# Block-sparse attention and gated MLP on one core: head 0's first queries transposed in fp32, copied in four chunks

## The chip, the cores and the metric

One core of a Trainium2 chip runs the whole program. The time is the device time of one execution in microseconds (us), the median of several. The engines of the core are named as the profile names them: PE (TensorE, the matrix products, with its weight loads listed as PEld), DVE (VectorE), ACT (ScalarE), POOL (GpSimd) and SP (SyncE, which issues most transfers). Each engine works through its own list of instructions in order, and waits at an instruction until what it needs has been signalled.

## The reference

```python
# attention: q, k, v are [4, 8, 768, 64], blocks of 32
scores = q @ k.T / 8
mask = |block_i - block_j| <= 1, or either block is the first or last,
       or block_j is one of three sampled blocks of block_i
attn = softmax(where(mask, scores, -1e9))
x = (attn @ v), heads side by side: [4, 768, 512]
# gated MLP with a spatial product
h = relu(x @ w_in)                      # 1024 columns
u, v = h[..., :512], h[..., 512:]
v_n = (v - mean(v)) / sqrt(var(v) + 1e-6)
v_s = w_spatial @ v_n + b_spatial       # along the sequence
out = (u * v_s) @ w_out
```

## The kernel before

Sixteen pairs of heads (four of each of the four batches) go through attention, and each batch then through the MLP. For one head the kernel keeps a tile `kq`: rows 0 to 63 hold the transposed keys (columns 0 to 767) and queries (columns 768 to 1535), rows 64 to 127 hold rows that carry the mask, one-hot block numbers under the keys and penalties under the queries. A product of 128 rows then gives score and mask at once. ACT turns each block of scores into exponentials (`a_all`), PE multiplies them with the values (`vv`), which carry a column of ones for the sum, and DVE divides.

Sequence positions are laid out so that each of the 128 partitions holds six neighbouring positions; a "chunk" is one of these six, and a transpose of two chunks of 64 columns at a time gives 128 rows: the first chunk in rows 0 to 63 and the second in rows 64 to 127 of the PSUM tile.

The schedule is written by hand: the order of the code is the order on each engine. Pair 0's heads are treated apart, since nothing can run before their data is there. Their first four chunks are loaded by `load` through ACT's queue (keys, then queries, of head 0), the rest through SP's. `cast` converts the staged fp32 tile `st_k` or `st_q` to the bf16 tile `nat`; for the first four chunks it also reorders them, so that one transpose yields chunks 0 and 2 and the other chunks 1 and 3, and rows 0 to 63 of the PSUM tile hold chunks 0 and 1 side by side (the first third of the queries, 256 columns) and rows 64 to 127 chunks 2 and 3. `head` issues these transposes, with `ident` as identity, and `split0` copies one half (`t` = 0 or 1) out of PSUM into `kq` on DVE. `make_identity` fills and selects on POOL.

`mask_rows(ps, t, copy, ...)` multiplies the penalty table `bm` with the one-hot rows for a third `t` of the queries and copies the result (64 rows, 256 columns) into head 0's `kq`. `rows(heads, columns, engine)` copies mask rows from head 0 to other heads. `filler` issues small products of no use that keep PE active. The step `casts` lets POOL work off `ORDER`, the casts of pair 1, 2, 3 and so on, and issues the loads that are four entries ahead; a staging buffer is loaded again when its cast is done.

Then the slots begin. Each `qk_unit` issues the score products of one block into one of two PSUM buffers `sc` and one exponential on ACT; the very first, of head 0, is issued in two halves (`ps` and `ps_f`), each with its own exponential. Other steps (transposes of later pairs, value products, later the MLP) are hung to slots by number.

Of the kernel before, what the change touches and what calls it, by code (L numbers as in the profile page):

```python
# [10 lines left out]
FP32 = mybir.dt.float32  # L11
# [15 lines left out]
def kernel(  # L27
# [16 lines left out]
    nc = tc.nc  # L44

    B, H, S, D = q.shape
# [16 lines left out]
    TC = NCH // NT  # L63
    TW = TC * 128
# [5 lines left out]
    const = ctx.enter_context(tc.tile_pool(name="const", bufs=1))  # L70
    work = ctx.enter_context(tc.tile_pool(name="work", bufs=1))
    psum = ctx.enter_context(tc.tile_pool(name="psum", bufs=1, space=bass.MemoryType.PSUM))
    ctx.enter_context(tc.manual_schedule())

    ident = const.tile([128, 128], BF16)
    warm = const.tile([128, 128], BF16)
    w_in_t = const.tile([128, NDM, DFF], BF16)
    w_out_t = const.tile([128, NDH, DM], BF16)
# [4 lines left out]
    kq = const.tile([128, H, 2 * S], BF16, name="kq")  # L83
    NVV = 6
    vv = [const.tile([128, 2, NCH, VA], BF16, name=f"vv{s}") for s in range(NVV)]
    MR = slice(D, KR)
    MX = slice(D, 128)
    K_, Q_ = slice(0, S), slice(S, 2 * S)

    def qcols(t0, n=1):  # L90
        return slice(S + t0 * TW, S + (t0 + n) * TW)


    st = {}
# [6 lines left out]
    H0, H1, BOTH = slice(0, 1), slice(1, 2), slice(0, 2)  # L101
    ALLC, C01, C03, C45 = slice(0, NCH), slice(0, TC), slice(0, 2 * TC), slice(2 * TC, NCH)
# [12 lines left out]
    def nat0_view():  # L115
        return nat[0].rearrange("p c h d -> p (c h d)").rearrange("p (h x) -> p h x", h=2)

    def cast(p, nm, eng, hs=BOTH, cs=ALLC):
        if nm == "v":
            dst = vv[p % NVV][:, hs, cs, 0:D]  # L120
        else:
            if p not in nat:
                nat[p] = work.tile([128, 2 * NCH, 2, D], BF16, tag="nat", bufs=4, name="nat")
            c0 = 0 if nm == "k" else NCH
            dst = nat[p][:, c0 + cs.start:c0 + cs.stop].rearrange("p c h d -> p h c d")[:, hs]
        src = st[nm, p].rearrange("p h (c d) -> p h c d", d=D)[:, hs, cs]
        if p == 0 and nm != "v":
            dst = nat0_view()[:, hs, (c0 + cs.start) * D:(c0 + cs.stop) * D]
            if cs is not C45:
                dst = dst[:, 0].rearrange("p (i t d) -> p t i d", t=2, d=D)  # L130
                src = src[:, 0].rearrange("p (t i) d -> p t i d", t=2)
            else:
                dst = dst.rearrange("p h (c d) -> p h c d", d=D)
        if eng is nc.scalar:
            nc.scalar.activation(out=dst, in_=src, func=AF.Copy)
        else:
            eng.tensor_copy(out=dst, in_=src)  # L137
# [23 lines left out]
    def iota(out, pattern, base, mult):  # L161
        nc.gpsimd.iota(out, pattern=pattern, base=base, channel_multiplier=mult,
                       allow_small_or_imprecise_dtypes=True)
# [2 lines left out]
    iota(edge[MR], [[0, 1]], 1 - NB, 2)  # L166
    iota(hot[MX], [[2, NCH], [2 * NCH, 128]], 1 - BLK, -2 * BLK)
    iota(col[MR], [[0, NR], [1, NB]], 0, 0)
    make_identity(nc, ident)
    for s in range(NVV):  # L170
        nc.gpsimd.memset(vv[s][:, :, :, D:VA], 1.0)
    nc.gpsimd.memset(mhalf, -0.5)
    nc.gpsimd.memset(kq[0:D, 1, 0:TW], 0.0)

    wps = psum.tile([128, 512], FP32, tag="av", bufs=2)

    def filler(n, to):
        for _ in range(n):
            nc.tensor.matmul(out=to[:, 0:128], lhsT=warm, rhs=warm, start=True, stop=True)
# [28 lines left out]
    PL, DV = nc.gpsimd, nc.vector  # L208
# [4 lines left out]
    def act_copy(o, i):  # L213
        nc.scalar.activation(out=o, in_=i, func=AF.Copy)
# [21 lines left out]
    def rows(hs, cs, eng=nc.vector):  # L236
        src = kq[MX, 0:1, cs].to_broadcast([MX.stop - MX.start, hs.stop - hs.start, cs.stop - cs.start])
        if eng is nc.scalar:
            nc.scalar.activation(out=kq[MX, hs, cs], in_=src, func=AF.Copy)
        else:  # L240
            eng.tensor_copy(out=kq[MX, hs, cs], in_=src)

    cast(0, "k", nc.scalar, H0, C03)
    act_copy(kq[MX, 0, K_], kq[MX, 1, K_])
    cast(0, "q", PL, H0, C03)
    cast(0, "k", PL, H0, C45)
    cast(0, "k", PL, H1)
    cast(0, "q", PL, H1, C03)
# [4 lines left out]
    def moe_tag():  # L253
        moe_tags.rotate(1)
        if moe_tags[0] in held:
            moe_tags.rotate(1)
        return moe_tags[0]

    def bank(nm="ps", tag=None):
        return psum.tile([128, 1024], BF16, tag=tag or moe_tag(), bufs=2 if tag else 1, name=nm)  # L260
# [7 lines left out]
    def mask_rows(ps, t, copy, h=0, rs=slice(0, KR)):  # L268
        nc.tensor.matmul(out=ps[:, 0:TW], lhsT=bm[rs], rhs=kq[rs, h, t * TW:(t + 1) * TW],
                         start=True, stop=True)  # L270
        copy(kq[MX, 0, qcols(t)], ps[0:MX.stop - MX.start, 0:TW])


    def head(ps, h, c0, n, at=0):
        for i in range(0, n, 2):
            nc.tensor.transpose(out=ps[:, at + i * 64:at + (i + 2) * 64],
                                in_=nat0_view()[:, h, (c0 + i) * D:(c0 + i + 2) * D],
                                identity=ident)

    def split0(ps, h, c0, n, t, copy=dve_copy):  # L280
        w = n * 64
        copy(kq[0:D, h, c0 * 128 + t * w:c0 * 128 + (t + 1) * w], ps[t * D:(t + 1) * D, 0:w])

    K4, K2, Q4 = (0, 2 * TC), (2 * TC, NCH - 2 * TC), (NCH, 2 * TC)
# [3 lines left out]
    rows(slice(3, 4), K_)  # L288
    filler(FILL2[0], wps)
    mask_rows(psum.tile([128, 1024], FP32, tag="sc", bufs=2, name="mq"), 0, act_copy, 1)  # L290
    rows(slice(2, 3), slice(0, 512), nc.scalar)
    filler(FILL2[1], wps)
    psq = bank("psq", "av")
    head(psq, 0, *Q4)
    split0(psq, 0, *Q4, 0)
    split0(ps0, 0, *K4, 1)
    filler(FILL2[2], wps)
    mask_rows(psum.tile([128, 512], FP32, tag=moe_tag(), bufs=1, name="mq"), 1, act_copy, rs=MR)
    split0(psq, 0, *Q4, 1)
    rows(slice(4, 6), K_)  # L300
    rows(H1, qcols(0, 2), PL)
    rows(slice(2, 3), slice(512, S), PL)

    ORDER = ("k1 q1a v00 v01 k2 q2a v1 k3 q3a v2 q1b q2b r v3 q3b q0c w00 w01 w02 w03 w10 w12 w11 w13").split()
    PIECE = {"k": {}, "v": {}, "q": {}, "a": {"cs": C01}, "b": {"cs": C25}, "c": {"cs": C45},
# [592 lines left out]
```

## Time and profile before

| what | value |
|---|---|
| median of 3 runs | 210.62 us (210.41 to 210.62) |
| the profiled execution | 210.04 us, of which its span is 208.3 us |
| PE busy | 201.0 us (97%) |
| ACT busy | 168.4 us (81%) |
| DVE busy | 146.8 us (70%) |
| POOL busy | 89.4 us (43%) |
| granted TensorE clock | 1.00 |

The span is the time from the first to the last recorded instruction; some 1.7 us of the execution lie around it. A view of the profile either lists groups of instructions (line, engine, operation, output and input tiles, shapes, count, busy time and the mean of one in ns, idle time before them with what ended it) or instructions in order of time (start, length, what). The chain of waits follows from the last instruction back to what released it, again and again. Matmuls are pipelined: one lasts longer than the distance to the next.

### The profile page before, as it was taken

The page shows a single profiled execution, that of the slowest core. Times are in us where ns is not written, and L with a number is a line of the kernel's source. Part 1 is how long each engine was busy: PE and PEld are TensorE (multiplying, and loading weights), DVE is VectorE, ACT ScalarE, POOL GpSimd, SP SyncE. Part 2 cuts the span into 40 slices and gives each one's busy share as a digit, 9 for nine tenths or more (in the row PEclk, how much of TensorE's full clock was granted, in tenths as well). Part 3 has the DMA queues.
Part 4 walks back from the last instruction along what each step waited for, and adds up shares of the span by engine and source line. Part 5 has one row for each costly group of instructions (what it writes and reads, how often), then busy time and mean ns, then how long its engine had stood idle before and what let it go on. Part 6 is the DMA issues. An engine that isn't in the chain of part 4 may idle for free.

```text
span 208.3 us, 5489 instructions
## 1 busy us (share of the span) xinstructions
PE 201.0 (97%) x2203; PEld 138.0 (66%) x2225; DVE 146.8 (70%) x315; ACT 168.4 (81%) x222; POOL 89.4 (43%) x186
## 2 busy tenths in 40 slices
PE   6899999999999999999999999999999999999993
PEld 6599888777766776667556676667665567445551
DVE  6888776989876766575975585456875666576871
ACT  6899999999999999989899878889899884266021
POOL 6888989767927964006757600006210000013000
PEclk9999999999999999999999999999999999999999
DMA  5999899999999999499987920499402010610016
GB/s 143 338 362 357 275 383 270 206 247 389 253 253 308 259 300 208 139 199 386 292 176 206 139 41 0 164 189 335 75 0 41 0 37 4 250 57 0 0 70 232
DMA packets 53053, 39.48 MB, mean 190 GB/s; under 512 B 33956, under 2 KB 47652, under 8 KB 53028
## 3 DMA queue, kind: packets, MB, share of 16 engines
q1 hardware_dynamic: 52596, 38.74, 70.0%
q10 hardware_dynamic: 432, 0.39, 0.6%
q8 instruction: 17, 0.28, 0.5%
q14 instruction: 8, 0.07, 0.1%
HBM read 24.77 MB, written 6.29 MB: 149 GB/s over the span
## 4 chain that ended last, share of the span: by engine, by line
PE 87%; DVE 4%; ACT 4%; DMA 2%; issue 1%; POOL 0%; ACTq 0%
PE ps L428 21%; PE ps_moe L630 17%; PE ps_moe L561 13%; PE ps_av L476 12%; PE ps L415 7%; PE ps_av L458 4%; PE ps_t L561 4%; PE ps_t L630 4%; PE ps_sc L630 2%; ACT a_all L420 2%; DVE stats L594 2%; DVE vn L185 2%; DMA st_q<-in_q_dram 2%; PE ps_sc L561 1%; PE ps L263 1%
## 5 line engine op out<-in xcount | busy, mean ns | idle before, releaser
L431 ACT ACTIVATE a_all<-ps 128x768 bf16<-128x768 f32 x144 | 113.4, 812 | 13.8 <-PE ps L428 6.2
L428 PE MATMUL ps<-kq 128*128 128x512 bf16 (+1 forms) x288 | 70.3, 326 | 0.3
L476 PEld LDWEIGHTS <-a_all 128*128 128x128 bf16 x864 | 46.6, 98 | 19.0
L476 PE MATMUL ps_av<-vv,a_all 128*128 128x65 bf16 x864 | 51.1, 194 | 0.1
L428 PEld LDWEIGHTS <-kq 128*128 128x128 bf16 x288 | 27.9, 97 | 23.6
L137 POOL CAST nat<-st_k 128x256 bf16<-128x256 f32 (+3 forms) x37 | 17.7, 509 | 38.7 <-DMA st_k<-in_k_dram 38.7
L420 ACT ACTIVATE a_all<-ps 128x1024 bf16<-128x1024 f32 x35 | 33.5, 1027 | 0.3
L630 PE MATMUL ps_moe<-w_spt,vn 128*128 128x512 bf16 (+1 forms) x144 | 33.1, 325 | 0.0
L598 POOL TENSOR_SCALAR std<-mv 128x3 f32<-128x3 f32 (+1 forms) x9 | 3.4, 376 | 48.7 <-DVE mv L595 48.5
L661 DVE TENSOR_TENSOR sb<-ps_moe,b_row 128x512 f32<-128x512 f32 x18 | 12.4, 690 | 14.5 <-PE ps_moe L630 14.2
L630 PE MATMUL ps_moe<-xt,w_in_t 128*128 128x256 bf16 (+1 forms) x108 | 21.7, 299 | 0.2
L415 PE MATMUL ps<-kq 128*128 128x256 bf16 x135 | 20.8, 275 | 0.8 <-DVE kq L211 0.6
L561 PE MATMUL ps_moe<-w_in_t,xt 128*128 128x512 bf16 x65 | 20.2, 378 | 0.2
L137 POOL CAST vv<-st_v 128x256 bf16<-128x256 f32 (+2 forms) x37 | 18.5, 533 | 3.9 <-DMA st_v<-in_v_dram 3.8
L137 POOL CAST nat<-st_q 128x256 bf16<-128x256 f32 (+2 forms) x41 | 19.2, 496 | 1.6 <-DMA st_q<-in_q_dram 1.5
L561 PE MATMUL ps_moe<-w_out_t,un 128*128 128x512 bf16 x64 | 19.4, 378 | 0.2
L441 DVE TENSOR_TENSOR xn<-ps_av,rc 128x384 bf16<-128x384 f32 (+1 forms) x36 | 18.5, 513 | 1.4 <-DVE rc L440 0.2
L664 DVE TENSOR_TENSOR un<-sb,un 128x512 bf16<-128x512 f32 x24 | 17.4, 727 | 1.5
L630 PEld LDWEIGHTS <-vn 128*128 128x128 bf16 x192 | 15.5, 97 | 4.4
L594 DVE BATCH_NORM_STATS2 stats<-vn 128x6 f32<-128x512 bf16 x24 | 16.5, 688 | 1.5 <-ACT vn L589 0.9
L211 DVE COPY osb<-ps_moe 128x512 f32<-128x512 f32 x12 | 8.3, 689 | 11.2 <-PE ps_moe L561 9.3
L211 DVE COPY kq<-tt 64x1536 bf16<-64x1536 bf16 x24 | 15.4, 641 | 0.6 <-DMA tt<-nat 0.2
(94 smaller groups left out, 241.6 us busy)
## 6 DMA issues: line engine op xcount, KB each, us to landing
out_dram<-osb SPq DMA_DIRECT2D x23, 256.0 KB, 2.1
st_k<-in_k_dram SPq DMA_DIRECT2D x15, 384.0 KB, 4.6
st_v<-in_v_dram SPq DMA_DIRECT2D x15, 384.0 KB, 6.2
st_q<-in_q_dram SPq DMA_DIRECT2D x12, 384.0 KB, 4.9
ws_f<-in_moe_w_spatial_dram SPq DMA_DIRECT2D x6, 384.0 KB, 5.5
w_f<-in_moe_w_in_dram SPq DMA_DIRECT2D x8, 256.0 KB, 6.3
w_f<-in_moe_w_out_dram SPq DMA_DIRECT2D x4, 256.0 KB, 5.4
st_q<-in_q_dram SPq DMA_DIRECT2D x3, 256.0 KB, 6.9
```

Of the source, the lines that this page charges most:

```text
L137: eng.tensor_copy(out=dst, in_=src)
L211: nc.vector.tensor_copy(out=o, in_=i)
L415: nc.tensor.matmul(out=ps[:, at:at + n * TW], lhsT=kq[:, h, ci * 128:(ci + 1) * 128], rhs=kq[:, h, qcols(t0, n)], start=True, stop=True)
L420: nc.scalar.activation(out=out, in_=ps, func=AF.Exp, scale=0.125)
L428: nc.tensor.matmul(out=ps[:, n0:n1], lhsT=kq[:, j % H, ci * 128:(ci + 1) * 128], rhs=kq[:, j % H, S + n0:S + n1], start=True, stop=True)
L431: nc.scalar.activation(out=a_ref["h", j][:, ci, :], in_=ps[:, 0:S], func=AF.Exp, scale=0.125)
L441: nc.vector.tensor_tensor(out=out, in0=ps[:, :, 0:D], in1=rc[:, 0:n].to_broadcast([128, n, D]), op=ALU.mult)
L476: nc.tensor.matmul(out=av_ref[j][:, qc, :], lhsT=a_ref["h", j][:, ci, qc * 128:(qc + 1) * 128], rhs=vv[p % NVV][:, h, ci, :], start=(ci == ...
L561: nc.tensor.matmul(out=ref["ps"][:, 0:w], lhsT=lhs(i), rhs=rhs(i), start=(i == 0), stop=(i == n - 1))
L594: nc.vector.bn_stats(out=stats, in_=self.vn[:, tcc, :])
L630: nc.tensor.matmul(out=o.rearrange("p (c t) -> p c t", c=n), lhsT=lhs(i)[:, (d0 + x) * 128:(d0 + x + 1) * 128], rhs=rhs(i), start=(i == 0) ...
L664: nc.vector.tensor_tensor(out=self.in_place(*area), in0=sb, in1=self.in_place(*area), op=ALU.mult)
```

## The change

The fp32 identity `ident_f` is made first and copied to the bf16 `ident` on POOL; the clearing of head 1's first query columns in `kq` moves ahead of the memsets of `vv`. Head 0's first four query chunks are no longer cast by POOL. PE transposes them from the staged fp32 tile `st_q`, two neighbouring chunks at a time, into an fp32 PSUM tile `psq`, and four copies of one chunk each (64 rows, 128 columns, `q_part`) bring them to `kq`: chunks 0 and 2 by DVE, 1 and 3 by ACT. The second `mask_rows` stands right behind the first, in an `sc` buffer. ACT's copy of 512 columns of mask rows to head 2 goes, and POOL's copy to that head covers all 768 columns instead of the last 256.

```diff
     ident = const.tile([128, 128], BF16)
+    ident_f = const.tile([128, 128], FP32)
...
-    make_identity(nc, ident)
+    make_identity(nc, ident_f)
+    nc.gpsimd.tensor_copy(out=ident, in_=ident_f)
+    nc.gpsimd.memset(kq[0:D, 1, 0:TW], 0.0)
     for s in range(NVV):
         nc.gpsimd.memset(vv[s][:, :, :, D:VA], 1.0)
     nc.gpsimd.memset(mhalf, -0.5)
-    nc.gpsimd.memset(kq[0:D, 1, 0:TW], 0.0)
...
     cast(0, "k", nc.scalar, H0, C03)
     act_copy(kq[MX, 0, K_], kq[MX, 1, K_])
-    cast(0, "q", PL, H0, C03)
     cast(0, "k", PL, H0, C45)
...
     mask_rows(psum.tile([128, 1024], FP32, tag="sc", bufs=2, name="mq"), 0, act_copy, 1)
-    rows(slice(2, 3), slice(0, 512), nc.scalar)
+    mask_rows(psum.tile([128, 1024], FP32, tag="sc", bufs=2, name="mq"), 1, act_copy, 1, MR)
     filler(FILL2[1], wps)
-    psq = bank("psq", "av")
-    head(psq, 0, *Q4)
-    split0(psq, 0, *Q4, 0)
+    psq = psum.tile([128, 512], FP32, tag="av", bufs=2, name="psq")
+    for i in range(TC):
+        nc.tensor.transpose(out=psq[:, i * 128:(i + 1) * 128],
+                            in_=st["q", 0][:, 0, 2 * i * D:2 * (i + 1) * D], identity=ident_f)
+
+    def q_part(c, copy):
+        r = c % 2 * D
+        copy(kq[0:D, 0, S + c * 128:S + (c + 1) * 128],
+             psq[r:r + D, c // 2 * 128:(c // 2 + 1) * 128])
+
+    q_part(0, dve_copy)
+    q_part(1, act_copy)
     split0(ps0, 0, *K4, 1)
     filler(FILL2[2], wps)
-    mask_rows(psum.tile([128, 512], FP32, tag=moe_tag(), bufs=1, name="mq"), 1, act_copy, rs=MR)
-    split0(psq, 0, *Q4, 1)
+    q_part(2, dve_copy)
+    q_part(3, act_copy)
     rows(slice(4, 6), K_)
     rows(H1, qcols(0, 2), PL)
-    rows(slice(2, 3), slice(512, S), PL)
+    rows(slice(2, 3), K_, PL)
```

## The prediction, made before the changed kernel had run

> **What bounds the kernel now.** I read the chain of waits first, because it says which work ends last and where it passes from engine to engine; then the busy time by stages; then the timeline of the first 12 us, which is all that the edits touch. The stages (columns: stretch, its length, busy time and instructions of each engine, granted clock, DMA share, GB/s):
>
> ```profile
> 4.50:6.10 1.60, 1.03 (x8) 0.53 (x9) 0.93 (x4) 1.06 (x3) 1.36 (x4) 1.00 0.82 239
> 6.10:11.00 4.90, 4.08 (x40) 2.88 (x41) 4.31 (x12) 4.89 (x7) 4.61 (x9) 1.00 1.04 349
> 11.00:40.00 29.00, 28.83 (x454) 25.72 (x457) 23.17 (x58) 28.66 (x31) 26.38 (x42) 1.00 1.08 311
> ```
>
> From 11.0 us on PE (first number) hardly rests: 28.83 of 29.00 us here, and 1.1 us of idle in all from 11 to 203 us. From 6.1 to 11.0 it is ACT (fourth) that never rests, 4.89 of 4.90. So a shift of ACT's first exponential moves everything behind it. The chain in the first 11 us (start, us, what):
>
> ```profile
> 1.14 3.19 DMA st_q<-in_q_dram
> 4.34 0.06 issue
> 4.39 0.57 POOL nat L137
> 4.97 0.04 issue
> 5.01 0.30 PE psq L276 x2
> 5.31 0.02 issue
> 5.34 0.30 DVE kq L211
> 5.63 0.04 issue
> 5.68 0.41 PE ps L407 x2
> 6.08 0.02 issue
> 6.11 1.09 ACT a_all L410 x2
> 7.19 3.77 ACT a_all L420 x4
> 10.96 0.04 issue
> 11.01 0.60 PE ps L415 x4
> ```
>
> Head 0's first queries land at 4.33; GpSimd casts, PE transposes, DVE copies, PE multiplies, and the first exponential starts at 6.11. That start is the quantity to predict; a handover costs 0.02 to 0.06 us.
>
> **The change part by part.** The unknown is X, the time from PE's start on the queries (4.39 as GpSimd's before, the landing being the same) to the end of both fp32 transposes.
>
> *The cast goes.* 0.57 us of GpSimd and one handover of 0.04 leave the chain.
>
> *The transposes become fp32.* No fp32 matmul is in the trace. Lower end: the bf16 pair, 0.30. In the built program the fp32 transpose is one instruction without the separate weight load that each bf16 one has, so I count its load as unhidden. A load takes 0.097 (first row below), a product follows the last by 0.056 (the row of eight: 0.61 less the 0.22 of one, over 7), and 0.16 (0.22 - 0.056) is the last one's latency. One load and one product each: X = 2 x 0.153 + 0.16 = 0.47. Upper end, four unhidden passes each: 2 x 4 x 0.153 + 0.16 = 1.38. I take 0.47, nearest to the bf16 row, since a transpose only moves data. The Trainium skill, "TensorE: Matmul & The Clock Gate", section Terms, says that Trainium2's weight loads and matmuls have a transpose mode that is four times faster for FP32; by it the sum goes with 0.47, and the passes end would not occur; no row here shows it.
>
> ```profile
> L428 PEld LDWEIGHTS <-kq 128*128 128x128 bf16 x288 | 27.9, 97 | 23.6
> 9.51 0.61 PE L263 MATMUL ps<-ident,nat 128*128 128x128 bf16 x8
> L211 DVE CAST kq<-mq 64x256 bf16<-64x256 f32 x1 | 0.4, 419 | 0.0
> L214 ACT ACTIVATE kq<-mq 64x256 bf16<-64x256 f32 x2 | 0.8, 377 | 0.5 <-PE mq L269 0.5
> 4.57 0.61 ACT L239 ACTIVATE kq<-kq 64x512 bf16<-64x512 bf16 x1
> 6.35 1.21 POOL L241 COPY kq<-kq 64x512 bf16<-64x512 bf16 x2
> ```
>
> *Four chunk copies for two copies.* The old 64x256 bf16 copy took 0.284; the new ones read fp32. DVE: 0.419 for 256 columns (CAST row), 0.689 for 512 (the osb copies), so 1.05 ns a column and 0.284 for 128. ACT: 0.377 for 256, and 0.595 against 1.027 for the exponentials of 512 and 1024 columns, 0.84 ns a column, so 0.269. The division looks parallel, but in the built program each copy waits for the one before it: chunk 1 (ACT) for DVE's chunk 0, chunk 2 for ACT, chunk 3 for DVE. The first exponential stands behind chunk 3 on ACT. With t = 4.39 + X: chunk 0 ends at t + 0.03 + 0.284, chunk 1 at t + 0.62, chunk 2 at t + 0.95, chunk 3 runs from t + 0.99. ACT starts the next instruction, if it waits for nothing, 0.1 before the last ends (the mask copy at 4.29 lasts 0.38, the row copy behind it starts at 4.57), so the first exponential starts at t + 0.99 + 0.17 = t + 1.16 = 5.55 + X. The scores are not later: chunk 1 lets PE start at t + 0.67, and 0.43 (6.11 - 5.68) on makes t + 1.10. Against 6.11 the shift is X - 0.56: -0.26, **-0.09**, +0.82 for the three X. On DVE, `split0` of the keys fits into the wait for chunk 1, and chunk 2 ends at 5.34 + X = 5.81 instead of 6.15, so what is queued behind (the 0.56 row copy, the later halves) comes sooner, not later. PE's products for the third exponential now wait for chunk 3 instead of DVE's copy (6.15): with X = 0.47 it ends at 4.86 + 1.26 = 6.12; they take 0.60, and that exponential starts at 7.08 at the earliest.
>
> *Second mask product and ACT's row copy.* The product moves from 5.34 to just behind the first (3.97); its copy, 0.377 on ACT, follows at about 4.57, where the row copy of 0.61 was, and ends by 4.95, before chunk 1 at 5.20. Cost nothing; the cover is PE's and ACT's wait for the queries, and without it 0.38.
>
> *GpSimd's row copy grows from 256 to 768 columns.* It took 0.40; 768 take 0.83 (the same copy at 25.54) to 1.3 (256 and 512 columns here took 0.40 and 0.86). The cast of head 1's queries ends at 6.29 as before, held by its DMA, so rows run 6.31 to 7.8 or 8.5 instead of to 7.56. The next cast waited for its DMA until 7.79: late by 0 to 0.7. Behind it stand pair 1's casts, which PE's transposes use at 9.40 (keys) and 9.75 (queries; their cast ended at 8.96), and the transfers that need those buffers back. At most 0.2 reaches PE at 9.75; ACT has some 0.2 in hand there. I take nothing.
>
> *Identity.* Fill and select once more in fp32, then a 128x128 copy (0.29, as the 128x128 cast): about 3.16 instead of 2.79, wanted by the key transposes at 3.62. The `kq` fill ends at about 3.5, wanted at 3.97. Nothing; uncovered it would be up to 0.4. The count memsets behind end by 4.2, and GpSimd's next cast waits for a DMA.
>
> Sum: -0.09 on the profiled execution's 210.04 (span 208.3 and 1.74 around it). The median of the three runs is 210.62, 0.58 above that execution; the same shift gives **210.5**.
>
> **The rivals.**
> - *fp32 takes several passes, unhidden.* X = 1.38, the first exponential at 6.93, +0.82: 211.4. For it: four bytes a value, and the one-instruction form. Against: overlapped, four passes would be 8 x 0.063 (the load pitch in a row of eight, 0.54 for 8) + 0.16 = 0.66, only +0.10. Slower by 0.42 begins at X = 0.98. The Trainium skill, "FP8 and Floating Point Precision", section TensorE Precision Notes, has true FP32 take four passes; it does not say this of transposes.
> - *fp32 costs what bf16 does.* X = 0.30, -0.26: 210.36. For it: the moving columns are as many. Against: the hidden load that bf16 has.
> - *GpSimd becomes late.* Rows to 8.5, pair 1's casts late by 0.7, and v3's transfer issued later by as much (SP waited for that buffer at 10.22): 0.2 at the transposes and as much again if a weight cast misses; 210.9. For it: GpSimd busy 4.61 of 4.90 us. Against: it waited 0.29 and 0.26 us for DMAs at 11.66 and 14.22, which takes such a lag back, and the first expert weights are cast some 1.3 us before PE uses them at 21.23.
> - *More is gained than the start.* Work that comes earlier fills part of PE's 1.1 us of later idle; -0.5: 210.1. For it: the idle is there. Against: no row ties it to the start.
> - *The copies run side by side, as they are written.* Two rounds of 0.28 instead of four, a start at 5.0 + X and a gain of 0.64 (209.98); the waits in the built program exclude it.
>
> **How the numbers follow.** Forecast 0.38 (210.4 to 210.8), several passes 0.30, bf16's price 0.14, GpSimd late 0.06, more gained 0.12. A measurement here can tell about 0.2%, 0.42 us, from no change. Faster: 0.12 and 0.04 of bf16's price with luck in the idle, 0.16. Slower: 0.30 and half of GpSimd late, 0.33. Within: 0.51. The time is the likeliest case's, 210.5. The range takes in the several passes and the gain at the other end, 210.1 to 211.5; the likeliest case alone has 210.4 to 210.8.
>
> **What would show it.** Transposes of psq starting near 4.39 and ending near 4.86; chunk copies one after the other, DVE near 4.89, ACT 5.21, DVE 5.52, ACT 5.85; first exponential near 6.02 instead of 6.11; ACT gapless to 10.9; PE without new idle at 9.4. Several passes show as psq ending past 5.4, GpSimd late as idle of PE before the transposes near 9.4 released by a cast. The prediction is wrong if the first exponential starts before 5.7 or after 6.5, or if its shift is not the shift of PE's block at 11.01.

## The result and the profile after

The changed kernel takes 210.82 us (median of 22 executions, 210.30 to 212.63), the kernel before 210.14 us (22 executions beside them, 209.79 to 210.62): ratio 1.0045, 95% interval 1.0033 to 1.0057. It is slower by 0.45%, where no change was forecast. The spread has grown as well: 7 of the 22 executions took 211.49 us or more, none of the 22 before. The ratio takes in that tail; the medians lie 0.68 us, 0.32%, apart.

The profiled execution took 211.07 us (span 209.3), 1.03 more than the 210.04 (span 208.3) before. The stages of the changed kernel, with the columns of the prediction (stretch, length, busy time and instructions of PE, PEld, DVE, ACT, POOL, granted clock, DMA share, GB/s):

```profile
4.50:6.10 1.60, 1.36 (x8) 0.91 (x8) 0.74 (x3) 0.80 (x3) 0.68 (x2) 1.00 0.81 257
6.10:11.00 4.90, 3.85 (x34) 2.72 (x34) 3.88 (x12) 4.51 (x8) 4.75 (x8) 1.00 1.03 352
```

Two things are to be seen. From 4.5 to 6.1 PE issues eight instructions as before, but is busy for 1.36 us instead of 1.03. And ACT, gapless from 6.1 to 11.0 before (4.89 of 4.90), now has 0.39 us of idle there. The chain of waits of the changed kernel (start, us, what) says where the first exponential went:

```profile
0.97 2.96 PE wps L181 x26
...
4.36 0.54 PE mq L270 x2
4.89 0.33 PE wps L181 x2
5.22 0.44 PE psq L296 x2
...
5.68 0.29 DVE kq L213
...
6.00 0.28 ACT kq L216
...
6.32 0.38 PE ps L417 x2
...
6.93 1.09 ACT a_all L420 x2
...
11.74 0.60 PE ps L425 x4
```

Before, this chain ran through the landing of the queries and GpSimd's cast. Now it is PE without a pause from 0.97 to 5.66: the fillers, the key transposes, both mask products (`mq` x2), fillers again, then the fp32 transposes. The first exponential starts at 6.93 instead of 6.11 (+0.82), PE's block at 11.74 instead of 11.01 (+0.73).

The transfer of the queries is no longer in the chain. It was issued at 1.14 us before and at 1.15 after, but landed sooner (the last number is the time from issue to landing, in us). Before:

```profile
st_q<-in_q_dram ACTq DMA_DIRECT2D x1, 128.0 KB, 3.2
```

After:

```profile
st_q<-in_q_dram ACTq DMA_DIRECT2D x1, 128.0 KB, 2.5
```

So the queries lay ready at 3.64 instead of 4.33, and PE came to them at 4.90. Over all 17 traces of this case the same transfer landed between 3.5 and 4.5 us, in 14 of them by 4.13: the trace of the kernel before that the prediction was made from is one of the three late ones.

PE's timeline shows why PE is late (start, us from the first to the last of a group, engine, line, what). Before:

```profile
3.71 0.28 PE L276 MATMUL ps<-ident,nat 128*128 128x128 bf16 x2
```

After:

```profile
3.72 0.42 PE L277 MATMUL ps<-ident,nat 128*128 128x128 bf16 x2
...
4.15 0.74 PE L270 MATMUL mq<-kq,bm 88*128 88x256 bf16 x2
4.82 0.39 PE L181 MATMUL wps<-warm 128*128 128x128 bf16 x2
5.01 0.64 PE L296 MATMUL psq<-ident_f,st_q 128*128 128x128 f32 x2
```

The same two key transposes last 0.28 us before and 0.42 after. A pair is one distance plus the length of one: 0.28 is 0.056 + 0.22, 0.42 is 0.107 + 0.31. So PE takes 128 columns every 0.107 us in the one execution where it takes them every 0.056 in the other. I call the first half pitch and the second full pitch. The granted clock reads 1.00 in both; the spacing alone shows it. Both executions begin at half pitch (26 fillers in 2.90 and 2.96 us). What differs is when full pitch begins: at 3.7 us in the profiled execution before, at 5.7 to 6.3 in the one after.

The Trainium skill, "TensorE: Matmul & The Clock Gate", Part 1, says that the array is clocked at half rate until one free-running activity window of about 3.4 us was busy, and gives 106.7 and 55.6 ns from start to start at 128 columns. The two spacings agree with the trace.

### The profile page after: what moved, and what is told of

Read it like the earlier page. It is cut to its first block, busy times and chain, and to the rows that moved or that the text cites. A ratio compares the mean times of both kernels' runs of the same rounds, so it can differ in the third digit from the quotient of the medians.

```text
span 209.3 us, 5515 instructions
## 1 busy us (share of the span) xinstructions
PE 203.3 (97%) x2225; PEld 138.8 (66%) x2225; DVE 147.7 (71%) x315; ACT 168.3 (80%) x223; POOL 89.4 (43%) x186
## 3 DMA queue, kind: packets, MB, share of 16 engines
HBM read 24.77 MB, written 6.29 MB: 148 GB/s over the span
## 4 chain that ended last, share of the span: by engine, by line
PE 95%; ACT 3%; DVE 0%; issue 0%; ACTq 0%
PE ps L438 22%; PE ps_moe L640 19%; PE ps_moe L571 15%; PE ps_av L486 13%; PE ps L425 6%; PE ps_av L468 4%; PE ps_t L571 4%; PE ps_t L640 4%; PE ps_sc L640 2%; ACT a_all L430 2%; PE wps L181 2%; PE ps_sc L571 1%; PE ps L264 1%; PE ps_av L264 1%; ACT a_all L420 1%; PE mq L270 0%
## 5 line engine op out<-in xcount | busy, mean ns | idle before, releaser
L608 POOL TENSOR_SCALAR std<-mv 128x3 f32<-128x3 f32 (+1 forms) x9 | 2.9, 318 | 49.1 <-DVE mv L605 48.5
L640 PE MATMUL ps_moe<-xt,w_in_t 128*128 128x256 bf16 (+1 forms) x112 | 22.9, 302 | 0.0
L571 PE MATMUL ps_moe<-w_in_t,xt 128*128 128x512 bf16 x72 | 22.3, 378 | 0.0
L425 PE MATMUL ps<-kq 128*128 128x256 bf16 (+1 forms) x136 | 21.0, 276 | 0.9 <-POOL nat L138 0.6
L571 PE MATMUL ps_moe<-w_out_t,un 128*128 128x512 bf16 x72 | 21.1, 378 | 0.0
L138 POOL CAST nat<-st_q 128x256 bf16<-128x256 f32 (+2 forms) x40 | 17.8, 472 | 0.8 <-DMA st_q<-in_q_dram 0.6
```

The costliest lines, as they stand in the source:

```text
L425: nc.tensor.matmul(out=ps[:, at:at + n * TW], lhsT=kq[:, h, ci * 128:(ci + 1) * 128], rhs=kq[:, h, qcols(t0, n)], start=True, stop=True)
L571: nc.tensor.matmul(out=ref["ps"][:, 0:w], lhsT=lhs(i), rhs=rhs(i), start=(i == 0), stop=(i == n - 1))
L640: nc.tensor.matmul(out=o.rearrange("p (c t) -> p c t", c=n), lhsT=lhs(i)[:, (d0 + x) * 128:(d0 + x + 1) * 128], rhs=rhs(i), start=(i == 0) ...
```

## The experiments

Sorted by what they ask. Every ratio is against the kernel before, timed on the same chip. (Its executions beside the later kernels went above 211.4 us in 1 of 35 and 1 of 29.) Full pitch is read from the spacing of the matmuls, to some 0.2 us; a range stands where no matmul ran in between.

| kernel | ratio [95%] | executions over 211.4 us | in the traced execution: queries landed, full pitch from, first exponential, time (us) |
|---|---|---|---|
| before | | 0 of 22 | 4.3, 3.7, 6.11, 210.04 |
| after | 1.0045 [1.0033, 1.0057] | 7 of 22 | 3.6, 5.7 to 6.3, 6.93, 211.07 |
| before_again | one execution | | 3.7, 6.8, 6.11, 210.65 |
| after_again | one execution | | 3.7, 5.4, 6.83, 211.13 |
| after_third | one execution | | 3.8, 4.3, 6.37, 210.35 |
| nofill2 | 1.0051 [1.0029, 1.0073] | 6 of 12 | 3.7, 9.4, 6.74, 211.67 |
| before_nofill | 1.0024 [1.0002, 1.0046] | 1 of 12 | 4.5, 9.9, 6.58, 212.08 |
| fill_gap | 1.0035 [1.0019, 1.0051] | 0 of 12 | 3.9, 6.7, 6.94, 211.31 |
| bf16_rest | 1.0036 [1.0014, 1.0058] | 4 of 12 | 3.6, 9.5 to 9.9, 6.78, 211.85 |
| rest_mask_back | 1.0012 [0.9989, 1.0036] | 2 of 12 | 4.4, 9.4 to 9.7, 6.66, 211.64 |
| mask_only | 1.0016 [1.0000, 1.0032] | 1 of 12 | 4.1, 4.5, 5.95, 210.19 |
| mask_late | 1.0011 [0.9996, 1.0026] | 0 of 11 | 3.7, 3.65, 6.41, 210.24 |
| psq_first | 1.0028 [1.0015, 1.0041] | 1 of 12 | 4.1, 10.1, 6.78, 211.63 |
| two_banks_fill | 1.0017 [0.9999, 1.0034] | 0 of 12 | 3.8, 5.5, 6.65, 210.50 |
| two_banks_first | 1.0013 [0.9999, 1.0026] | 0 of 12 | 4.0, 5.5, 6.49, 210.40 |
| two_banks_swap | 1.0009 [0.9996, 1.0022] | 0 of 11 | 4.1, 3.65, 5.75, 209.87 |

### Is it the execution or the kernel? before_again, after_again, after_third

The two kernels unchanged, traced again.

> The kernel before, unchanged, for a second trace. Theory A (PE's matmuls run at half pitch, 0.107 us a 128-column filler instead of 0.056, until a moment that differs between executions, and the changed kernel has more PE work ahead of its first exponential): the fillers' pitch changes at another time than 3.7 us; if it is later, the query transposes take 0.42 instead of 0.30 and the first exponential moves from 6.11 to 6.3-6.6. Theory B (the cost is only the price of the fp32 transposes and of the four copies in series): first exponential at 6.1 whatever the pitch.

> The changed kernel, unchanged, for a second trace. Theory A: if the pitch changes by 4 us, the query transposes start at 4.4 to 4.6, take less than 0.76 and the first exponential is at 6.1 to 6.4, time near 210.3; if it changes later, as in the first trace (5.5 or after), they start at 4.9 and the first exponential is at 6.9 or later, 211 and more. Theory B: psq and the first exponential stand at 4.9 and 6.9 again, 210.8.

> The changed kernel once more, for the moment of the full pitch and the time that goes with it. Theory D, by the traces so far (full pitch from 5.4 to 6.9 us: 210.5 to 211.3; after 9: 211.6 and more): full pitch by 4.5 gives 210.3 or less with the transposes starting by 4.7 and ending by 5.2, full pitch between 5 and 7 gives 210.6 to 211.2, after 9 gives 211.6 and more.

Full pitch begins at another time in each. before_again ran at half pitch up to 6.8 us, and its first exponential still started at 6.11:

```profile
4.15 0.42 PE L269 MATMUL mq<-kq,bm 88*128 88x256 bf16 x1
...
4.58 0.42 PE L276 MATMUL psq<-ident,nat 128*128 128x128 bf16 x2
...
6.11 0.60 ACT L410 ACTIVATE a_all<-ps 128x512 bf16<-128x512 f32 x1 [0.16 <-PE ps L407]
```

6.3 to 6.6 had been expected at half pitch. The equal 6.11 does not show that the old order tolerates it: the queries landed at 3.73 in this execution, not 4.33, and GpSimd had cast them by 4.19. The transposes began 0.43 us sooner (4.58 for 5.01), and the way from there to the exponential took as much longer (1.53 for 1.10). Where the queries came late and PE was at half pitch, the old path had its exponential at 6.58 (before_nofill) and 6.66 (rest_mask_back). (The 210.65 us of before_again go with a later wait: head 1's queries were cast by 6.70 instead of 6.29, and the copies of DVE ahead of the scores at 8.73 ended at 8.67 instead of 8.31.)

In the three traces of the changed kernel the queries landed by 3.76, 0.9 to 1.3 us before PE came to them, so PE was the later one in each. There, the sooner full pitch begins the sooner is the first exponential: 6.93, 6.83 and 6.37. In after_third, at full pitch from 4.3, PE's timeline has them at:

```profile
4.69 0.39 PE L296 MATMUL psq<-ident_f,st_q 128*128 128x128 f32 x2
```

Even there the transposes end at 5.08, not 4.86, since the mask products and fillers ahead of them still end later than 4.39. late_pairs below begins with the same program; it was at half pitch until past its transposes, and has 6.93 again. Within the changed kernel these are four executions and no more; neither the pitch nor the landing was set by hand.

### What does a pair of fp32 transposes cost? late_pairs

Two needless pairs were put into slots 10 and 12 of the changed kernel, where PE runs at full pitch. Its 212.08 us contains them and isn't used.

```diff
+    def pairs():
+        ps = psum.tile([128, 512], FP32, tag=moe_tag(), bufs=1, name="ps_x")
+        for i in range(2):
+            nc.tensor.transpose(out=ps[:, i * 128:(i + 1) * 128], in_=ident_f, identity=ident_f)
+    when(10, pairs)
+    when(12, pairs)
```

> The changed kernel with two more pairs of fp32 transposes (of the identity, their result unused) in slots 10 and 12, some 16 to 18 us into the span, where matmuls have run at full pitch in every trace so far: the price of a pair by itself. At half pitch the pair took 0.75 us from its first weight load to its end (4.90 to 5.65). Theory A and D: it is the clock, so the pair takes 0.4 to 0.5 here, as the sum of the prediction had it (0.47). Theory B: fp32 is the price; 0.7 or more here too.

The view of the tile in late_pairs (durations in ns: least, median, most):

```profile
L848 PEld LDWEIGHTS ps_x<-ident_f x4: 143/143/145, 16.3 to 18.7; 128*128 128x128 f32 x4
L848 PE MATMUL ps_x<-ident_f x4: 273/288/305, 16.3 to 18.8; 128*128 128x128 f32 x4
```

The same view of the changed kernel's own pair (its loads took 227):

```profile
L296 PE MATMUL psq<-ident_f,st_q x2: 421/421/421, 5.0 to 5.2; 128*128 128x128 f32 x2
```

From the first load to the end the first late pair takes 0.44 us (16.31 to 16.75), the one at 4.90 takes 0.74 (to 5.64). Forecast were 0.47, or 1.38 with four unhidden passes, or 0.66 with four overlapped ones. So the pair costs what was forecast, and the pitch does the rest; four passes are out, hidden or not.

The terms of the 0.47 were not right, though. An fp32 transpose starts the next product 0.21 us after itself at half pitch (5.01, 5.22, 5.44) and 0.11 to 0.14 at full pitch, twice the 0.107 and 0.056 of a bf16 product of 128 columns. And the second load begins beside the first product (16.37 and 16.34), where the prediction counted it as unhidden. A product twice as long and a hidden load nearly cancel.

### Do the fillers matter? nofill2, fill_gap, before_nofill

```diff
-    FILL, FILL2 = 26, (2, 2, 2)
+    FILL, FILL2 = 26, (0, 0, 0)
```

This is nofill2, made from the changed kernel, and before_nofill, made from the one before. fill_gap is the changed kernel with `(2, 2, 6)`.

> The changed kernel without the three pairs of fillers between its first steps. Theory A: with half pitch PE reaches the query transposes some 0.2 to 0.4 sooner, so 210.4 to 210.6, unless less PE activity makes the half pitch last longer, which would show as fillers and transposes of 0.107 pitch past 6 us and a slower time. Theory B: psq is set by the transfer that lands at 4.3 and by the copies behind it; 210.8 as the changed kernel.

> The changed kernel with six fillers instead of two behind the fp32 transposes, so that PE works while the four copies run. Theory D (PE starts at half pitch; the full pitch comes at the end of a window of some 3.4 us, only if PE was active enough in it; the changed kernel leaves PE idle for 0.5 to 0.7 us before its first scores and fails one more window in about a third of its executions): no execution, or at most one in twelve, above 211.5; median 210.3 to 210.6. Theory A (only the later place of the steps at half pitch counts): the same spread as the changed kernel, a third of the executions above 211.5, median 210.8.

> The kernel before without its three pairs of fillers. Theory D: less PE activity lets it fail a window as the changed kernel does, so some executions (2 to 6 of 12) above 211.2 and a wider spread than 209.8 to 210.6; median 210.3 to 211. Theory A: the fillers only stand in PE's way; 209.9 to 210.1 without a tail.

Without fillers, PE reaches the transposes sooner, and yet nothing is won: 6 of 12 executions of nofill2 are over 211.4 us, and in its trace full pitch begins only at 9.4. In all traces full pitch begins either between 3.65 and 6.8 us or between 9.4 and 10.2, never between. The traced executions with the late start took 211.63 to 212.08 us, the others without added work at most 211.31, so the changed kernel's executions above 211.4 are probably such ones; none of them was caught in a trace. The Trainium skill, "TensorE: Matmul & The Clock Gate", Part 1, describes a free-running window of about 3.4 us. The two groups agree with that: the first is 3.15 us wide, no more than one such window, and 9.4 to 10.2 lies one behind 6.0 to 6.8. That they come from it is not shown.

Four fillers more in PE's wait for the copies (fill_gap) leave no execution above 211.33, but the median stays at 210.92: they mend the tail and not the shift. The median expected for it was too low. before_nofill lies above 211.4 only once, less than expected, though its traced execution was one of the late ones. That PE's idle time in the first microseconds delays full pitch is supported by fill_gap (0 of 12 against 7 of 22); 6 of 12 for nofill2 could be chance, before_nofill speaks rather against it, and how much idle time it takes stays open.

### Which edit carries it? bf16_rest, rest_mask_back, mask_only, mask_late, psq_first

bf16_rest is the changed kernel with the old path of the queries (cast, bf16 transposes, two copies); the rest of the change stays.

```diff
+    cast(0, "q", PL, H0, C03)
...
-    psq = psum.tile([128, 512], FP32, tag="av", bufs=2, name="psq")
...
-    q_part(0, dve_copy)
-    q_part(1, act_copy)
+    psq = bank("psq", "av")
+    head(psq, 0, *Q4)
+    split0(psq, 0, *Q4, 0)
...
-    q_part(2, dve_copy)
-    q_part(3, act_copy)
+    split0(psq, 0, *Q4, 1)
```

rest_mask_back puts the second `mask_rows` of that kernel behind `filler(FILL2[2], wps)`. mask_only is the kernel before with the second `mask_rows` moved right behind the first, into an `sc` buffer, and nothing else. mask_late is the changed kernel with it moved back:

```diff
-    mask_rows(psum.tile([128, 1024], FP32, tag="sc", bufs=2, name="mq"), 1, act_copy, 1, MR)
     filler(FILL2[1], wps)
...
     filler(FILL2[2], wps)
+    mask_rows(psum.tile([128, 1024], FP32, tag="sc", bufs=2, name="mq"), 1, act_copy, 1, MR)
     q_part(2, dve_copy)
```

psq_first has it directly behind the fp32 transposes, ahead of the copies, with `FILL2 = (2, 0, 4)`.

> The change without its fp32 transposes and chunk copies: GpSimd casts the queries and two copies follow as before; identity, second mask product, and row copies as in the changed kernel. Theory A and B: the fp32 way is the cost, so the time is that of the kernel before, within 0.3 us. Rival C (the second mask product ahead of the transposes, or GpSimd's larger row copy, is the cost): 210.6 to 210.9, as the changed kernel.

> The change without fp32 transposes and chunk copies, as bf16_rest, but the second mask product back behind the query transposes; of the change, the identity, the order of the fills and the row copies remain. Theory D: with PE's wait filled as before, no tail, 209.9 to 210.3. Rival E (the tail comes from GpSimd's identity copy, which makes the mask table late, or from the row copies): a tail above 211.5 in a third of the executions, 210.6, as bf16_rest.

> The kernel before with one edit of the change alone: the second mask product right behind the first, ahead of the query transposes, in an sc buffer; ACT's row copy stays, behind both mask copies. Theory D (the product costs about 0.3 us of PE at half pitch ahead of the transposes, and no longer fills PE's wait before the first scores): ratio 1.002 to 1.0035, some executions above 211.2, as bf16_rest. Rival E (the identity copy and the row copies are the cost): ratio 1.000 within 0.001.

> The changed kernel with the second mask product back behind the query transposes; its copy on ACT then stands between the copies of chunks 1 and 3. Theory D: the transposes start about 0.3 sooner at half pitch, but the mask copy of 0.28 to 0.38 stands ahead of chunk 3 and the first exponential; together 0.1 to 0.3 better than the changed kernel, ratio 1.002 to 1.0035. If the copies in series were all of the cost: 1.0045 or more, since one more is in the series.

> The changed kernel with the fp32 transposes ahead of the second mask product and of its fillers, and four fillers behind. Theory A and D: at half pitch PE reaches the transposes at about 4.6 instead of 4.9 and works on while the copies run, so some 0.3 sooner and no execution above 211.5: 210.4 to 210.6. Theory B: the place does not matter, 210.8.

bf16_rest keeps 1.0036 without any fp32 transpose, as its rival C had it. Its traced execution also shows why a late full pitch costs more than the start: ACT stands still for PE's score products at half pitch (from 7.07), 0.30 us ahead of the third exponential and 0.36 ahead of the next, at 9.55.

```profile
7.07 1.06 PE L416 MATMUL ps<-kq 128*128 128x256 bf16 x4
...
8.17 1.02 ACT L421 ACTIVATE a_all<-ps 128x1024 bf16<-128x1024 f32 x1 [0.30 <-PE ps L416]
```

Its mask products came late besides (4.44 instead of 4.15): DVE's last step for the penalty table took 0.53 us there, beside GpSimd's cast of the queries, and 0.19 in the trace of the changed kernel.

Against that, mask_late keeps the fp32 transposes and the four copies and comes to 1.0011; its interval (to 1.0026) and that of the changed kernel (from 1.0033) don't touch. So the second mask product's place ahead of the transposes carries a good part of the loss: three quarters by the ratio, and the tail (0 of 11 above 211.4), but only half by the medians (+0.35 us stay of +0.68). That is the only pair that tells by itself: rest_mask_back against bf16_rest overlaps, psq_first overlaps with both, and mask_only alone is barely off zero and below what was expected (1.002), though 3 of its 12 executions lie above 211.2, against 1 of the 29 beside it. The tails of rest_mask_back and psq_first (2 and 1 of 12) were not expected.

mask_late shows a second thing. It ran at full pitch from 3.65 and its transposes began at 4.33, close to the forecast 4.39, and still its first exponential started at 6.41, not 6.02 (its timeline):

```profile
4.33 0.39 PE L295 MATMUL psq<-ident_f,st_q 128*128 128x128 f32 x2
4.35 0.51 POOL L138 CAST nat<-st_k 128x384 bf16<-128x384 f32 x1 [0.17 <-DMA st_k<-in_k_dram]
4.38 0.69 DVE L243 COPY kq<-kq 64x768 bf16<-64x768 bf16 x1
```

DVE's row copy to head 3 took 0.69 beside GpSimd's cast of head 1's keys, which began 0.03 earlier; in the two main traces, where DVE began first, it took 0.36. It stands ahead of the first chunk copy, which so starts at 5.10 instead of the forecast 4.89: 0.21 of the 0.39. The rest is ACT's mask copy, now ahead of chunk 3, and an exponential that starts only after chunk 3 has ended. The cast starts there because its transfer landed at 4.29 (at 4.75 in the trace of the changed kernel) and GpSimd no longer has the queries ahead of it.

### Can the copies run side by side? two_banks_fill, two_banks_first, two_banks_swap

Each pair of chunks gets a PSUM tile of its own, and each engine copies one of them whole, in place of the four `q_part`:

```diff
+    psr = psum.tile([128, 512], FP32, tag=moe_tag(), bufs=1, name="psr")
+    for c in range(2 * TC):
+        nc.tensor.transpose(out=(psq, psr)[c // 2][0:D, c % 2 * 128:(c % 2 + 1) * 128],
+                            in_=st["q", 0][:, 0, c * D:(c + 1) * D], identity=ident_f)
...
+    def q_half(t, ps, copy):
+        copy(kq[0:D, 0, qcols(t)], ps[0:D, 0:TW])
+
+    q_half(0, psq, dve_copy)
+    q_half(1, psr, act_copy)
```

two_banks_fill has `FILL2 = (2, 2, 4)`; two_banks_first `(2, 0, 4)` and the second `mask_rows` behind the transposes; two_banks_swap has it behind the copies as well.

> The changed kernel with each fp32 transpose of one chunk instead of two, chunks 0 and 1 into one PSUM tile, 2 and 3 into another, so that DVE copies one of 256 columns and ACT the other at the same time, and four fillers behind. Theory D together with the price of the copies in series: DVE's copy 0.42, the first scores at 0.5 and the first exponential at 0.95 behind the transposes instead of 1.2 to 1.3, no tail; 209.8 to 210.2. Theory B (fp32 is the price): four transposes instead of two cost 0.2 to 0.45 more, 210.6 to 211.2.

> Both repairs together: the fp32 transposes ahead of the second mask product, one chunk each into two PSUM tiles, one copy by DVE and one by ACT at the same time, fillers behind. Theory D with the price of the copies in series: first exponential at 6.2 to 6.4 at half pitch, no execution above 211.3; 209.9 to 210.2, level with the kernel before or a little under it. Theory B: 210.5, as two_banks_fill.

> As two_banks_first, with ACT's copy of the second queries ahead of that of the second mask product. In the trace of two_banks_first the first exponential (6.49) waited for ACT's copies, 5.80 and 6.21, while its scores began at 5.93; with the order swapped ACT is free at 6.1 to 6.2 and the scores end at 6.3, so 0.1 to 0.2 sooner: ratio 0.9995 to 1.0005, level with the kernel before.

The timeline of two_banks_fill:

```profile
5.68 0.42 DVE L213 CAST kq<-psq 64x256 bf16<-64x256 f32 x1 [0.61 <-PE psq L297]
...
5.91 0.38 ACT L216 ACTIVATE kq<-psr 64x256 bf16<-64x256 f32 x1 [0.61 <-PE psr L297]
```

With two tiles the copies overlap. From DVE's first copy to the first exponential it is 0.97 us (5.68 to 6.65) instead of 1.25 (5.68 to 6.93). The medians (210.51, 210.44, 210.25) are above what was expected, though, and none is below the kernel before. two_banks_swap has the earliest first exponential of all, 5.75, but PE's block starts at 10.85, 0.16 sooner than before and not 0.36. Its chain runs, in place of ACT, through the casts of head 1's keys and queries and their transposes:

```profile
6.27 0.41 POOL nat L138
...
10.85 0.60 PE ps L423 x4
```

So an earlier first exponential of head 0 pays only until the third waits for other data. The best version found is level with the kernel before (1.0009, interval 0.9996 to 1.0022), not better.

## Why the prediction was wrong

Forecast was a shift of -0.09 us, written as 210.5 on the 210.62 of three executions. Measured is +1.03 between the two profiled executions and +0.68 between the medians. The kernel before has 210.14 over 22 executions, so 210.82 lies nearer to 210.5 than the forecast deserves.

**The step that failed** is the one on the second mask product: "Cost nothing; the cover is PE's and ACT's wait for the queries, and without it 0.38", together with X counted "from PE's start on the queries (4.39 as GpSimd's before, the landing being the same)". In the traced execution PE has no such wait. The queries land at 3.64, but at half pitch PE is still at the mask products at 4.39, and comes to the queries at 4.90. The second mask product is 0.43 of this delay: before_again, at half pitch too and with one product ahead, has its first transpose at 4.58, the changed kernel at 5.01. (At half pitch the step from each of the two products to the next one is 0.35 and 0.32; the single one in before_again takes 0.21.) The 0.38 had been priced for ACT, whose part of the cover held: its two mask copies end at 5.30, chunk 1 starts at 6.00. The mistake was to think that PE had the cover too. At full pitch it would hardly have it either, by an estimate: mask_late, at full pitch from 3.65 and without the product ahead, has its first transpose at 4.33, and the product takes 0.21 to the next instruction in after_third, at full pitch; together about 4.5. After the change, PE waits later instead, for the copies.

The shift of the first exponential against the forecast, 6.93 - 6.02 = 0.91, goes by steps: 0.51 is the start of the transposes (4.90 for 4.39), 0.27 the pair itself (0.74 for 0.47), 0.13 the way from its end to the exponential (1.29 for 1.16). How much of the +0.68 between the medians each of them is, one trace cannot tell; moving the mask product back took away half of it.

- *The chain.* Right: the first exponential's start sets what follows, +0.82 there and +0.73 at PE's block. The span is 1.0 longer. The rest comes soon after: ACT's exponentials are 0.74 later at 13.7 us of the kernel before, 0.86 at 15.6 and 1.04 at 24.0, and it stays at that to the last copy (204.75 and 205.79). Why PE fell back there, by waits of 0.1 to 0.2 us, was not followed up.
- *X.* 0.47 was right for full pitch (0.44), partly by luck, since a product twice as long and a hidden load nearly cancel, and wrong for the stage; bf16's price, 0.30, is out at either pitch. The several passes, the rival at 211.4, had the first exponential at 6.93, where it came, for another reason: that is luck too.
- *The landing.* Taken to be the same, it was 0.7 us sooner. This did not matter, since PE was later still.
- *The chunk copies.* DVE 0.28 and ACT 0.27, one after the other, as forecast. ACT's start 0.1 ahead of the end of the last copy did not come: chunk 3 ends at 6.91 and the exponential starts at 6.93.
- *Identity.* Ready at 3.38, not 3.16, since its copy took 0.52 instead of 0.29; the key transposes came after it anyway. Beside it DVE's small comparison for the penalty table took 0.32 instead of 0.22, and the table was ready 0.13 later. At half pitch PE reaches the mask product at 4.15, where that no longer shows.
- *GpSimd's row copy.* The next cast at 8.17 instead of 7.79, within the bounds given. The profile names that cast for a wait of PE that ends at 9.08, but copies of DVE that PE needs ended there too (8.98), and in the kernel before the same products started (8.37) ahead of the cast's end (8.61). So no cost of it is seen on PE.
- *The old order's cover.* With the queries at 4.33, GpSimd's cast ends at 4.96, and PE at half pitch would have been there in time (4.47 in before_again, for its first weight load). So, by this estimate from two traces, the cast that was taken out of the chain would also have hidden a late PE; in the traces of the changed kernel the first exponential goes with the start of full pitch.

The half pitch was to be seen in the kernel before: its 26 fillers take 2.90 us, 0.107 from one to the next without the last one's latency (2.90 less 0.22, over 25), where the row of eight shown in the prediction has 0.056.

## What to carry to other kernels

Price work at the pitch of the place where it will stand: read the distance of equal matmuls in a row, there, in more than one execution, and not the granted clock alone. Read the landing of a transfer in more than one execution too. Before a slow step is cut out of a chain, ask which other engine arrives only just in time behind it; keep work that isn't needed first behind the first transposes, where it fills PE's wait. Two engines that copy halves of one PSUM tile took turns in this kernel, with two tiles they overlapped; and an early edit of under 1 us is judged by the spread of many executions, since single ones here differ by 2 us.

## What the runs showed of the hardware

- The start of full pitch varies from execution to execution of the same kernel (4.3, 5.4 and 5.7 to 6.3 us in three of the changed kernel), and falls in two groups over all traces, 3.65 to 6.8 and 9.4 to 10.2 us. The granted clock reads 1.00 from the start of the span in the two main traces.
- The same 128 KB transfer, issued at 1.14 or 1.15 us, landed between 3.53 and 4.49 us in 17 traces.
- An fp32 transpose of 128x128 has a load of 143 ns and a matmul of 273 to 305 ns at full pitch, 227 and 421 at half pitch. It holds up the next product twice as long as a bf16 one does: 0.21 us against 0.107 at half pitch, 0.11 to 0.14 against 0.056 at full pitch.
- DVE's 64x768 copy took 0.36 us when it began before GpSimd's cast and 0.69 when it began 0.03 after. The Trainium skill, "SBUF — State Buffer", section "SBUF: two separate sides", says that where an instruction of DVE uses the port pair that it shares with GpSimd, the engine that starts first holds the pair for its whole instruction; the two cases agree with that.
